# A fused attention, FFN and MoE kernel: four float64 weight chunks start their conversion on GpSimd, and the first block's order is rewritten

## The chip, the cores and the metric

The kernel runs on one core of one Trainium2 chip. The metric is the device time of one execution in microseconds (us), the median of three runs. The engines are TensorE (PE in the rows; PEld is its weight load), VectorE (DVE), ScalarE (ACT), GpSimd (POOL) and SyncE (SP), which here only starts transfers.

## The reference, cut to what matters

```python
scores = q @ k.T / sqrt(D); keep = is_global | is_local          # B=2, H=8, S=768, D=64
a = softmax(where(keep, scores - slope * dist, -1e9)); x = a @ v # -> x: 1536 x 512
h = x @ w_in                                                     # w_in: 512 x 2048
y = (h * tanh(softplus(h))) @ w_out                              # w_out: 2048 x 512
for e in range(4):                                               # four experts of width 1024
    out += p[:, e] * (relu(y @ w1[e]) @ w2[e])
```

All of it is to be float32, but `w_in` and `w_out` arrive as float64: the setup multiplies float32 random numbers by a float64 scalar. [...]

## The kernel before

The 1536 tokens are handled in three blocks of 512. A block goes through attention, the FFN (16 chunks of 128 hidden columns) and the experts. The later blocks overlap the attention of one block with the experts of another. The first block has nothing to overlap with, and this case is about it: `first_block` (line 788) issues its instructions in an order that is written out by hand, the string `PLAN` (line 42). Each letter is one step; the first occurrence of a letter is its step 0, the second its step 1, and so on, and the engines execute their own instructions in that order. I write a step as a letter and a number.

Attention of the first block has 16 pairs of heads. For pair k:

- S (TensorE): scores. X (VectorE, line 263): bias, and the row minimum, read from PSUM. E (ScalarE, line 274): exponentials. D (VectorE, lines 364 and 365): the inverse sums of two pairs.
- N (GpSimd) or V (VectorE), both line 370: the scaling of the probabilities, two instructions for a pair. T (TensorE): their transposes. C (ScalarE) or Z (VectorE), both line 380: the copy of the transposes out of PSUM. A (TensorE): probabilities times values.
- F (ScalarE) or G (VectorE), line 396: the copy of four pairs' results out of PSUM into `x0`, the input of the FFN.

Of the FFN of the first block, chunk c has the following steps.

- The raw chunk is 128 partitions x 1024 float64 (1 MB). It is fetched on SP's queue (line 563) into one of four buffers (`TURN`); two of them held queries and keys before. Chunk 0 is fetched at the very start, chunks 1 to 3 during attention, and chunk c+4 only when chunk c has been narrowed. The last two reuse buffers of chunks 12 and 13.
- a (ScalarE, line 584): reads every second 32-bit word, the upper half of each float64, scales it and writes float32. Three t steps (VectorE: line 587, then lines 589 and 591, which have two inputs from SBUF each) set the exponent and the mantissa. After the third t, SP writes the result to DRAM for the later blocks (line 593) and then starts the next fetch.
- H (TensorE, line 750): the hidden chunk. Then the activation `h * tanh(softplus(h))`: e (ScalarE exponential, line 643), c, n (VectorE), l (ScalarE logarithm and exponential, lines 662 and 663), u, m, v, g (VectorE, lines 667 to 682). P (TensorE, line 762): the product with `w_out`, accumulated over the 16 chunks.

At the end, w splits three expert chunks for the steps that follow, i and j and the digits begin block 1, and after P15 ScalarE and VectorE copy the result out (lines 743 and 744).

GpSimd has no instruction between 25.4 us and 152.6 us in the profile below. A step that waits holds up all that is behind it on its own engine: a waits for a fetch, and e and l stand behind it on ScalarE.

Of the kernel before, what the change touches and what calls it, by code (L numbers as in the profile page):

```python
# [12 lines left out]
AF = mybir.ActivationFunctionType  # L13
ALU = mybir.AluOpType

P = 128
# [8 lines left out]
NF1 = 16  # L25
# [6 lines left out]
TO_F32 = 2.0 ** -112  # L32
# [7 lines left out]


PLAN = (
    "SSYXXESYSEXSEDXNXESNTDCTXSENAZNEXATTSCZEDAXANSFSNEXTTDCNEZAXANTETSCZaADXNAtSFNTEXSCTXEAZSEDAVSVaXTTX"
    "CSEZAEADVVFTXTCEZAAaDVVTtTCaAZtAFtHtttteHcatntlHteaumcvnegacPtltumtHvngtlPteuamvcHgntltaPeucmtvgHntl"
    "tauPetmvgcPntltauHtmvgtePcnatltHutmteHvcagntltPeumavgHcntltuPetmcvnHgtlutPmevgcntlPumvgHtttePtcnlHau"
    "mtvtaHgetictnPetlcutHmwvgnwlPweuwcmvgHnwlwuwmPevcgnwlwPumvgj1P23456"
)

AFTER = {
# [473 lines left out]
class Body:  # L523
# [43 lines left out]
        self.w32[s] = self.wpool.tile([P, 1024], F32, tag="w", name=f"w{s}")  # L567
        self.nc.sync.dma_start(self.w32[s], (self.wts if kind == "moe" else self.wfirst if self.wide else self.wff)[n])

    def narrow(self, s):  # L570

        if s not in self.w64:
            return
        nc, raw = self.nc, self.w64.pop(s)
        word = raw.bitcast(I32).rearrange("p (n t) -> p n t", t=2)
        top = raw.bitcast(F32).rearrange("p (n t) -> p n t", t=2)[:, :, 1]
        if self.first:

            m = self.w32[s] = self.ring.tile([P, 1024], F32, tag="wl" if s % 2 else "wh", name=f"w{s}")
        else:
            m = self.w32[s] = self.wpool.tile([P, 1024], F32, tag="w", name=f"w{s}")
        nc.scalar.activation(m, top, AF.Abs, scale=TO_F32)
        yield
        mi = m.bitcast(I32)
        nc.vector.tensor_scalar(mi, mi, 0x0FFFFFFF, 3, ALU.bitwise_and, ALU.logical_shift_left)
        yield
        nc.vector.scalar_tensor_tensor(mi, word[:, :, 1], -0x40000000, mi, ALU.bitwise_and, ALU.bitwise_or)  # L589
        yield  # L590
        nc.vector.scalar_tensor_tensor(mi, word[:, :, 0], 29, mi, ALU.logical_shift_right, ALU.bitwise_or)
        if self.first:
            nc.sync.dma_start(self.wfirst[s], m)
# [194 lines left out]
    def first_block(self, ready, now):  # L788


        nc = self.nc
        pairs = [FirstPair(self, k) for k in range(TB // P * NP)]
        then = Attention(self, self.pair, 1)
        n = dict.fromkeys("SXEDNTCAFHecnlumvgPatw", 0)
        narrowing = [self.narrow(c) for c in range(NF1)]
        parts = [self.part(c) for c in range(NF1, NF1 + 3)]
        self.x0 = self.xy.tile([P, KC, TB], F32, tag="xyh", name="x0")

        for pair in pairs:
            pair.load()  # L800
            if pair.n == 9:
                now("fetch", 2)

        def ahead():
            while ready["fetch"] < NF1:
                c = ready["fetch"]
                before = [m for m in range(c) if TURN[m] == TURN[c]][-1:]
                if n["S"] < FREE.get(TURN[c], 0) or any(n["t"] < 3 * m + 3 for m in before):
                    break
                now("fetch", c + 1)  # L810

        def scores(k):
            pairs[k].scores()
            ahead()

        def warm(k):

            nc.tensor.matmul(self.bank(f"warm{k}", 0), self.ident, self.ident.unsqueeze(1).to_broadcast([P, 4, P]), start=True, stop=True)

        def inverse(k):  # L820
            assert n["E"] >= 2 * k + 2
            pairs[2 * k].inverse()

        def scale(engine):
            def run(k):
                assert n["D"] > k // 2
                pairs[k].scale(engine)
            return run

        def take(engine):  # L830
            def run(k):
                assert n["A"] >= 4 * k + 4
                pairs[4 * k].take(engine)
                ahead()
            return run

        def hidden(s):
            if s == 4:
                for c in range(NF1, NF1 + 3):
                    self.fetch(c)  # L840
            assert n["F"] == 4 and n["t"] >= 3 * s + 3
            self.accumulating = True
            self.hidden_first(s)
            ahead()

        def project(s):
            self.project_first(s)

        def begin(c):
            assert (c < 2 or n["A"] >= min(2 * c - 2, len(pairs))) and (c < 10 or n["P"] > c - 10)  # L850
            next(narrowing[c])

        def convert(k):
            c = k // 3
            assert n["a"] > c
            next(narrowing[c], None)
            ahead()

        def part(k):
            c, third = divmod(k, 3)  # L860
            assert ready["fetch"] >= NF1 and n["S"] == len(pairs) and n["P"] >= 8 + 2 * c
            if third == 0:
                ready["fetch"] = NF1 + 3
                next(parts[c])
            try:
                parts[c].send("vector" if third else None)
            except StopIteration:
                pass

        def begin_next(k):  # L870
            assert n["t"] >= 36
            then.load(4)

        pair = lambda stage, *args: lambda k: getattr(pairs[k], stage)(*args)
        ops = {
            "S": scores, "X": pair("biased"), "E": pair("exps"), "D": inverse, "N": scale(nc.gpsimd), "V": scale(nc.vector), "T": pair("trans"),
            "C": pair("copy", nc.scalar.copy), "Z": pair("copy", nc.vector.tensor_copy), "A": pair("av"),
            "F": take(nc.scalar.copy), "G": take(nc.vector.tensor_copy), "a": begin, "t": convert, "w": part,
            "Y": warm, "H": hidden, "e": self.mish_exp, "c": self.mish_cap, "n": self.mish_n, "l": self.mish_r,
            "u": self.mish_u, "m": self.mish_m, "v": self.mish_v, "g": self.gate_first, "P": project,  # L880
            "i": begin_next, "j": lambda k: then.split(k + 1),
            "1": lambda k: then.ahead(), "2": lambda k: then.scores(), "3": lambda k: then.softmax(),
            "4": lambda k: then.norm(), "5": lambda k: then.trans(), "6": lambda k: then.av(),
        }
        same = dict(Z="C", G="F", V="N")
        for token in PLAN:
            kind = same.get(token, token)
            for other in AFTER.get(kind, ()):
                assert n[other] > n[kind], (token, n[kind], other)
            ops[token](n.setdefault(kind, 0))  # L890
            n[kind] += 1
        ready["narrow"], ready["part"] = NF1, NF1 + n["w"] // 3
        return then, n["P"]
# [160 lines left out]
```

## Time and profile before

| | |
|---|---|
| median of 3 runs | 933.07 us (932.06 to 934.48) |
| the profiled execution: its own time | 934.25 us |
| the profiled execution: span in the profile | 932.4 us |
| busy over the span: TensorE, VectorE | 902.5 us, 532.8 us |
| busy over the span: ScalarE, GpSimd | 438.6 us, 370.3 us |
| mean granted TensorE clock | 0.993 |
| first block (to its last activation step) | 0 to 153.35 us |

The span runs from the first to the last instruction. Busy times are unions of an engine's instructions. Shares over the whole span mix two stages: from about 158 us on TensorE is busy almost without a gap, and before that it is not. The change lies in the first 153 us.

### The profile page before, as it was taken

Reading aid. Unit: us, or ns where it says so; the run is one execution under the profiler, and the core shown is the slowest. Engines: PE = TensorE matmul, PEld = TensorE weight load, DVE = VectorE, ACT = ScalarE, POOL = GpSimd, SP = SyncE. Lnnn points to the kernel's source line nnn. Section 1 sums busy time; section 2 is a strip of 40 time slices with the busy share of each in tenths; the row PEclk is TensorE's granted clock in tenths of the full one; section 3 lists DMA queues with packets and bytes.
Section 4 is the critical chain, followed back from the end, with each engine's and each line's share of the span. In section 5 each row is a group of like instructions: output and inputs, shape, how many; then the busy total and the mean of one; then the engine's idle time right before and its main releaser. Section 6 shows DMA issues by size and latency. Waiting matters only on the chain.

```text
span 932.4 us, 11519 instructions
## 1 busy us (share of the span) xinstructions
PE 902.5 (97%) x3962; PEld 689.6 (74%) x3962; DVE 532.8 (57%) x1057; ACT 438.6 (47%) x856; POOL 370.3 (40%) x379
## 2 busy tenths in 40 slices
PE   7889999999899999999999999999999999999997
PEld 4534444777688888877777888888888888888886
DVE  6989989776752188888777611248885121112122
ACT  6553436766553355666666643224445323423230
POOL 4000001775674445446766654400014444544440
PEclk9999999999899999999999999999999999999999
DMA  8477363534222578854444222055563243223201
GB/s 299 188 277 268 142 237 125 181 136 136 90 69 99 205 266 301 308 203 155 136 140 154 91 91 91 23 191 205 190 232 107 91 144 105 91 93 112 91 23 50
DMA packets 40373, 142.96 MB, mean 153 GB/s; under 512 B 4592, under 2 KB 7408, under 8 KB 38256
## 3 DMA queue, kind: packets, MB, share of 16 engines
q1 hardware_dynamic: 40160, 142.10, 43.2%
q8 instruction: 33, 0.54, 0.2%
q14 instruction: 36, 0.29, 0.1%
q10 hardware_dynamic: 144, 0.02, 0.0%
HBM read 113.80 MB, written 28.31 MB: 152 GB/s over the span
## 4 chain that ended last, share of the span: by engine, by line
PE 64%; DVE 19%; ACT 8%; DMA 4%; issue 3%; SPq 0%; POOL 0%; ACTq 0%; DVEq 0%; POOLq 0%
PE h L627 30%; PE acc L733 29%; DMA raw<-in_wff 2%; DVE kl L230 2%; DVE nr L672 2%; DVE e L667 2%; PE o L296 1%; DMA big<-in_wff 1%; ACT p L274 1%; PE pt L191 1%; DVE nr L678 1%; DVE w L589 1%; DVE n L655 1%; DVE e L682 1%; ACT wh L609 1%
## 5 line engine op out<-in xcount | busy, mean ns | idle before, releaser
L612 POOL TENSOR_TENSOR wl<-w,wh 128x512 fp32r<-128x512 f32 x218 | 289.7, 1350 | 324.5 <-ACT wh L609 312.1
L708 DVE SCALAR_TENSOR_TENSOR gl<-h,gh 128x512 fp32r<-128x512 f32 x96 | 66.2, 690 | 267.3 <-ACT gh L703 267.3
L609 ACT CAST wh<-w 128x1024 fp32r<-128x1024 f32 x112 | 117.6, 1050 | 113.6 <-PE acc L733 106.2
L733 PE MATMUL acc<-wh,gh 128*128 128x512 f32 (+1 forms) x384 | 151.3, 394 | 0.0
L733 PE MATMUL acc<-wh,gl 128*128 128x512 f32 (+1 forms) x384 | 148.9, 388 | 0.0
L733 PE MATMUL acc<-wl,gh 128*128 128x512 f32 (+1 forms) x384 | 148.8, 387 | 0.0
L703 ACT ACTIVATE gh<-h 128x512 fp32r<-128x512 f32 x96 | 57.3, 597 | 115.7 <-PE h L627 115.7
L733 PEld LDWEIGHTS acc<-wh,gl 128*128 128x128 f32 x384 | 72.1, 188 | 15.1
L733 PEld LDWEIGHTS acc<-wl,gh 128*128 128x128 f32 x384 | 72.2, 188 | 14.2
L733 PEld LDWEIGHTS acc<-wh,gh 128*128 128x128 f32 x384 | 72.2, 188 | 13.9
L239 POOL TENSOR_TENSOR v<-raw,v 128x256 fp32r<-128x256 f32 x32 | 27.4, 855 | 127.2 <-ACT v L238 127.2
L750 PE MATMUL h<-x,w 128*128 128x512 f32 x128 | 57.0, 593 | 0.7 <-ACT x L396 0.7
L186 POOL TENSOR_SCALAR p<-p,st 128x256 f32<-128x256 f32 (+1 forms) x64 | 30.0, 481 | 65.1 <-DVE st L184 63.8
L627 PE MATMUL h<-y0h,wh 128*128 128x512 f32 x128 | 52.8, 413 | 2.4 <-DVE st L263 1.5
L274 ACT ACTIVATE p<-t,st 128x256 f32<-128x256 f32 (+1 forms) x96 | 46.3, 484 | 13.7 <-DVE st L263 13.3
L627 PE MATMUL h<-y0l,wh 128*128 128x512 f32 x128 | 51.0, 399 | 0.0
L627 PE MATMUL h<-y0h,wl 128*128 128x512 f32 x128 | 51.0, 398 | 0.0
L627 PE MATMUL h<-y1h,wh 128*128 128x512 f32 x128 | 50.8, 397 | 0.1
L627 PE MATMUL h<-y1l,wh 128*128 128x512 f32 x128 | 49.9, 390 | 0.0
L733 PE MATMUL acc<-gh,wh 128*128 128x512 f32 x128 | 49.9, 390 | 0.0
L627 PE MATMUL h<-y1h,wl 128*128 128x512 f32 x128 | 49.9, 390 | 0.0
L627 PE MATMUL h<-y2h,wh 128*128 128x512 f32 x128 | 49.9, 390 | 0.0
(154 smaller groups left out, 1795.3 us busy)
## 6 DMA issues: line engine op xcount, KB each, us to landing
w<-in_wts SPq DMA_DIRECT2D x96, 512.0 KB, 3.5
raw<-in_qkv SPq DMA_DIRECT2D x32, 512.0 KB, 3.7
big<-in_wff SPq DMA_DIRECT2D x10, 1024.0 KB, 6.7
wfirst<-w SPq DMA_DIRECT2D x16, 512.0 KB, 3.0
w<-wfirst SPq DMA_DIRECT2D x16, 512.0 KB, 4.2
wkeep<-wh SPq DMA_DIRECT2D x16, 512.0 KB, 3.1
wkeep<-wl SPq DMA_DIRECT2D x16, 512.0 KB, 2.9
wh<-wkeep SPq DMA_DIRECT2D x16, 512.0 KB, 3.2
```

The costliest lines, as they stand in the source:

```text
L186: nc.gpsimd.tensor_scalar(self.p[:, j, 0:self.nk * P], self.p[:, j, 0:self.nk * P], st[:, 2 + j:3 + j], 0.0, ALU.mult, ALU.add)
L230: nc.vector.tensor_tensor(self.kl, self.k, self.kh.bitcast(F32), ALU.subtract)
L239: nc.gpsimd.tensor_tensor(vv[:, :, 1:3, :], v, vv.bitcast(F32)[:, :, 0:4:3, :], ALU.subtract)
L274: nc.scalar.activation(p[:, j, 0:n], t[:, j, 0:n], AF.Exp, bias=self.least[:, j:j + 1], scale=-1.0, accum_out=self.sum[:, j:j + 1])
L609: (nc.vector.tensor_copy if copy == "vector" else nc.scalar.copy)(hi, w)
L612: getattr(nc, engine or "gpsimd").tensor_tensor(lo[:, c], w[:, c], hi.bitcast(F32)[:, c], ALU.subtract)
L627: nc.tensor.matmul(ps, a[:, c], r[:, kc, :], start=m == 0, stop=m == 3 * KC - 1)
L667: nc.vector.scalar_tensor_tensor(e, n, 2.0, r, ALU.add, ALU.mult)
L703: self.nc.scalar.activation(gh, self.h[s], AF.Relu)
L708: nc.vector.scalar_tensor_tensor(gl, h, 0.0, gh.bitcast(F32), ALU.max, ALU.subtract)
L733: nc.tensor.matmul(acc[:, h], a, r, start=f == 0 and m == 0, stop=f == per - 1 and m == 2)
L750: self.nc.tensor.matmul(ps, self.w32[s][:, kc * P:(kc + 1) * P], self.x0[:, kc, :], start=kc == 0, stop=kc == KC - 1)
```

## The change

`narrow` gets an argument. If it is set, the first conversion instruction runs on GpSimd as a multiplication instead of on ScalarE. The sign bit, which the absolute value cleared, is cut off by the next step's mask anyway. A new letter q begins a chunk in that way; a still begins it on ScalarE. The new `PLAN` uses q for chunks 0 to 3, has 16 C and no Z, four G and no F, eight N and eight V (before: eight C, eight Z, four F, ten N, six V), and another order nearly throughout. The number of each other letter is the same.

```diff
 PLAN = (
-    "SSYXXESYSEXSEDXNXESNTDCTXSENAZNEXATTSCZEDAXANSFSNEXTTDCNEZAXANTETSCZaADXNAtSFNTEXSCTXEAZSEDAVSVaXTTX"
-    "CSEZAEADVVFTXTCEZAAaDVVTtTCaAZtAFtHtttteHcatntlHteaumcvnegacPtltumtHvngtlPteuamvcHgntltaPeucmtvgHntl"
-    "tauPetmvgcPntltauHtmvgtePcnatltHutmteHvcagntltPeumavgHcntltuPetmcvnHgtlutPmevgcntlPumvgHtttePtcnlHau"
-    "mtvtaHgetictnPetlcutHmwvgnwlPweuwcmvgHnwlwuwmPevcgnwlwPumvgj1P23456"
+    "SSYXXESYSEXSEDXNXESNTDCTXSENANTCXSCqEAATSDCEXNAGSENXTCTDXNACtESNAEXTqTCDSCVAVEXATGETSCDSCVVAXqAXETTt"
+    "CSCAXEqASGEDXVEVTTCDCVAVAtTTCtCAtAGtHttatHectntlHeuacmvangetPlctumvHgntltaPeucmvnHgltauPmetvcgHntlt"
+    "umPetavcgnPtltutaHmtvtgeHtcantlPteucmvaHngtltuPetmvcHgnatlttPeumvgcPtntltHumtvteHgctntlPeuacmvHgntlt"
+    "auPemvgcnPtiltutHmtvwgwePwcwnwlwHuwmwvwgeHcnluPemvcgnlPumvgj1P23456"
 )
...
-    def narrow(self, s):
+    def narrow(self, s, gpsimd=()):
...
-        nc.scalar.activation(m, top, AF.Abs, scale=TO_F32)
+        if gpsimd:
+
+            nc.gpsimd.tensor_scalar(m, top, TO_F32, 0.0, ALU.mult, ALU.add)
+        else:
+            nc.scalar.activation(m, top, AF.Abs, scale=TO_F32)
...
-        narrowing = [self.narrow(c) for c in range(NF1)]
+        on_gpsimd = []
+        narrowing = [self.narrow(c, on_gpsimd) for c in range(NF1)]
...
-        def begin(c):
-            assert (c < 2 or n["A"] >= min(2 * c - 2, len(pairs))) and (c < 10 or n["P"] > c - 10)
-            next(narrowing[c])
+        def begin(gpsimd):
+            def run(c):
+                assert (c < 2 or n["A"] >= min(2 * c - 2, len(pairs))) and (c < 10 or n["P"] > c - 10)
+                on_gpsimd[:] = [c] * gpsimd
+                next(narrowing[c])
+            return run
...
-            "F": take(nc.scalar.copy), "G": take(nc.vector.tensor_copy), "a": begin, "t": convert, "w": part,
+            "F": take(nc.scalar.copy), "G": take(nc.vector.tensor_copy), "a": begin(0), "q": begin(1), "t": convert, "w": part,
...
-        same = dict(Z="C", G="F", V="N")
+        same = dict(Z="C", G="F", V="N", q="a")
```

## Rows read from the trace of the kernel before

**Rows 1.** Busy time of each engine in stretches; PEclk is TensorE's granted clock.

```profile
23.17:39.05 15.88, 13.55 (x132) 8.97 (x128) 14.09 (x50) 12.93 (x35) 2.19 (x4) 1.00 0.32 131
39.05:56.92 17.87, 15.06 (x31) 6.55 (x32) 14.38 (x20) 7.53 (x11) 0.00 (x0) 0.90 0.80 299
56.92:153.35 96.43, 94.27 (x218) 40.78 (x216) 90.13 (x128) 39.51 (x58) 0.73 (x1) 1.00 0.55 201
```

**Rows 2.** VectorE's waits from 23.17 to 153.35 us: total, times, longest.

```profile
DVE e L667 <- ACT r L663: 6.4, 9, 2.2
DVE e L650 <- ACT e L643: 1.2, 2, 0.9
DVE t L263 <- PE s L353: 1.1, 3, 0.6
DVE w L587 <- ACT w L584: 0.8, 1, 0.8
DVE st L364 <- ACT p L274: 0.7, 2, 0.4
```

**Rows 3.** Groups of VectorE's instructions, 23.17 to 153.35 us: busy us, mean ns.

```profile
L591 DVE SCALAR_TENSOR_TENSOR w<-big,w 128x1024 int32<-128x1024 int32 x10 | 12.2, 1221 | 0.1
...
L587 DVE TENSOR_SCALAR w<-w 128x1024 int32<-128x1024 int32 x16 | 11.0, 688 | 0.8 <-ACT w L584 0.8
...
L370 DVE TENSOR_SCALAR p<-p,st 128x256 f32<-128x256 f32 x12 | 3.4, 350 | 0.2
L380 DVE COPY pt<-pt 128x512 f32<-128x512 f32 x4 | 2.8, 688 | 0.0
```

**Rows 4.** Timeline, 18 to 24 us: start, duration, [idle before, releaser].

```profile
18.04 0.42 DVE L263 CUSTOM_DVE_ANT_0 t<-s,bias 128x256 f32<-128x256 f32 x1 [2.12 <-PE s L353]
...
22.33 0.70 PE L353 MATMUL s<-qk 64*128 64x256 f32 x4 [0.54 <-DMA qk<-in_qk]
...
23.17 0.42 DVE L263 CUSTOM_DVE_ANT_0 t<-s,bias 128x256 f32<-128x256 f32 x1 [0.37 <-PE s L353]
```

**Rows 5.** Line 380 on ScalarE: ns least, median, most; first and last start.

```profile
L380 ACT COPY pt<-pt x8: 354/585/585, 12.4 to 36.4; 128x512 f32<-128x512 f32 x6, 128x256 f32<-128x256 f32 x2
```

**Rows 6.** GpSimd: four scalings in the timeline, and line 612 as Rows 5.

```profile
15.43 1.84 POOL L370 TENSOR_SCALAR p<-p,st 128x256 f32<-128x256 f32 x4 [1.45 <-DVE st L365]
...
L612 POOL TENSOR_TENSOR wl<-w,wh x218: 1265/1289/1749, 165.9 to 907.5; 128x512 fp32r<-128x512 f32 x109
```

**Rows 7.** Timeline: one VectorE line alone and beside GpSimd.

```profile
153.83 0.69 DVE L230 TENSOR_TENSOR kl<-raw,kh 128x512 fp32r<-128x512 f32 x1
...
250.44 1.67 DVE L230 TENSOR_TENSOR kl<-raw,kh 128x512 fp32r<-128x512 f32 x1
...
248.83 2.73 POOL L612 TENSOR_TENSOR wl<-w,wh 128x512 fp32r<-128x512 f32 x2 [0.27 <-ACT wh L609]
```

**Rows 8.** Timeline of fetches of chunks 4 and 6, their a steps, and line 563's landings.

```profile
39.51 0.38 SPq L563 DMA_DIRECT2D big<-in_wff  x1
...
46.46 1.18 ACT L584 ACTIVATE w<-big 128x1024 f32<-128x1024 f32 x1 [2.80 <-DMA big<-in_wff]
...
45.97 0.37 SPq L563 DMA_DIRECT2D raw<-in_wff  x1
...
54.59 1.13 ACT L584 ACTIVATE w<-raw 128x1024 f32<-128x1024 f32 x1 [2.09 <-DMA raw<-in_wff]
...
56.92 0.69 DVE L667 SCALAR_TENSOR_TENSOR e<-n,r 128x512 f32<-128x512 f32 x1 [2.23 <-ACT r L663]
...
DMA to landing us min/median/max: 5.2/6.5/11.0
```

**Rows 9.** Timeline of VectorE: two steps u, and the last g.

```profile
125.48 0.69 DVE L667 SCALAR_TENSOR_TENSOR e<-n,r 128x512 f32<-128x512 f32 x1 [1.35 <-ACT r L663]
...
140.65 0.69 DVE L667 SCALAR_TENSOR_TENSOR e<-n,r 128x512 f32<-128x512 f32 x1 [0.15 <-ACT r L663]
...
152.66 0.69 DVE L682 TENSOR_TENSOR gl<-r,h 128x512 f32<-128x512 f32 x1
```

More of the change, by code (lines that the diff above doesn't have):

```diff
@@ L42 @@
 PLAN = (
-    "SSYXXESYSEXSEDXNXESNTDCTXSENAZNEXATTSCZEDAXANSFSNEXTTDCNEZAXANTETSCZaADXNAtSFNTEXSCTXEAZSEDAVSVaXTTX"
-    "CSEZAEADVVFTXTCEZAAaDVVTtTCaAZtAFtHtttteHcatntlHteaumcvnegacPtltumtHvngtlPteuamvcHgntltaPeucmtvgHntl"
-    "tauPetmvgcPntltauHtmvgtePcnatltHutmteHvcagntltPeumavgHcntltuPetmcvnHgtlutPmevgcntlPumvgHtttePtcnlHau"
-    "mtvtaHgetictnPetlcutHmwvgnwlPweuwcmvgHnwlwuwmPevcgnwlwPumvgj1P23456"
+    "SSYXXESYSEXSEDXNXESNTDCTXSENANTCXSCqEAATSDCEXNAGSENXTCTDXNACtESNAEXTqTCDSCVAVEXATGETSCDSCVVAXqAXETTt"
+    "CSCAXEqASGEDXVEVTTCDCVAVAtTTCtCAtAGtHttatHectntlHeuacmvangetPlctumvHgntltaPeucmvnHgtltauPmetvcgHntlt"
+    "umPetavcgnPtltutaHmtvtgeHtcantlPteucmvaHngtltuPetmcvgHnatlttPeumvgcPtntltHumtvteHgctntlPeuacmvHgntlt"
+    "auPemvgcnPtiltutHmtvwgwePwcwnwlwHuwmwvwgeHcnluPemvcgnlPumvgj1P23456"
 )
```

## The prediction

> **What bounds the kernel now.** I read the busy time by stretches first. From 23.17 us to the end of the first block VectorE is busy for 14.09 + 14.38 + 90.13 = 118.6 of 130.2 us [rows 1]; ScalarE is busy for less than half of the time and GpSimd has nothing to do. TensorE shows as busy as VectorE, but its bars include waiting in a filled pipeline; what ends last is told by the waits. VectorE stands still for 11.6 us in all, of which the view of its waits names 10.2 us [rows 2], and 7.6 of these end with ScalarE: a step u that waits for l, or a step c that waits for e. So in this stage VectorE's own work sets the time, plus about 10 us in which ScalarE's answer comes too late. From about 158 us on the order of this change plays no part, so what the first block gains or loses I carry to the end one to one.
>
> The clock of this argument starts at X10. The scores of pair 10 waited for their queries and keys, which landed at 22.33, and VectorE's X10 follows at 23.17 [rows 4]. That transfer is queued by the loads ahead of the written order, so the change can't bring it forward. Ahead of it VectorE has slack (2.12 us before X8 alone [rows 4]).
>
> **The work on VectorE.** The new order has no Z (-8 copies), four G (+4 copies of 512 columns) and two more V. Over the whole block this is a saving, but only what lies behind X10 counts. Before, Z9, Z11, Z13, Z15, six V and t0 lie behind X10. After, G1, G2, G3, eight V and D4 do, and t0 has moved ahead of it. Terms:
>
> - four Z gone: 4 x 0.69 = -2.75 by line 380 [rows 3]
> - t0 gone ahead: -0.69 by line 587 [rows 3]
> - G1 to G3: the same read of 512 columns of PSUM, 3 x 0.69 = +2.06 [rows 3]
> - V8 and V9, which were N8 and N9 on GpSimd: 4 x 0.35 = +1.40 [rows 3]
> - D4: two instructions on four columns, put at +0.3, less than half of such a copy, because it has almost no columns.
>
> Sum +0.3 us. The four other Z, which looked like a gain, lay where VectorE waits for the queries and keys anyway. All other VectorE steps are the same in number.
>
> **What goes to ScalarE.** Eight more C at 0.585 each at most [rows 5] and four F and four a fewer (a takes 1.18 [rows 8]): it ends with less work than before. It was busy for 12.93 of the 15.88 us behind X10 [rows 1], and there it now has ten C where it had F1 to F3, a0 to a3 and four C; this covers the extra copies. Without that cover each C would hold up its A by 0.6 us.
>
> **q on GpSimd.** Nothing of before shows a 1024-column scaling there. Four 256-column ones take 1.84 us, and two two-input halves 2 x 1.29 = 2.58 [rows 6]. The nearer row is the first, the same operation with four starts instead of one; so I take 1.5 us, between 1.1 (if about half of each 0.46 us scaling is its start; an estimate from that row) and 2.6. q0 stands ahead of N4 on GpSimd's queue; N4 must wait for D2 in both versions, and T4 behind it waits for the late X8, which covers it. q1 to q3 have no N behind them. Their results are wanted by t3, t6 and t9, more than 10 us of VectorE work later. So their duration itself costs nothing.
>
> What they can cost is VectorE's time. Line 230 on VectorE takes 0.69 us alone and 1.67 us while GpSimd runs a pair of 1.3 us instructions: about 1 us lost to one instruction [rows 7]. X, G and the copies read PSUM; V and t read SBUF, and q2 and q3 (their chunks land in the middle of the attention part) meet V10, V11 and perhaps t1. Bounds: 0 if they meet none, 2 x 2.58 = 5.2 if both are lost in full to V or t. I take 0.6, since X12 and X13 stand in the same stretch.
>
> The Trainium skill, SBUF — State Buffer, section "Who interferes with whom", says that VectorE and GpSimd share a pair of SBUF ports which one instruction holds for its whole length, and that a VectorE instruction with two SBUF inputs or in a two-port mode stops for a GpSimd instruction that reads SBUF. It speaks against this change, and line 230 agrees with it. By it the upper bound would be the price whenever q starts first.
>
> **The waits.** Now what is late next. The end of t2 releases chunk 4's fetch. Before, it was issued at 39.51 and a4 began at 46.46, 6.95 us later [rows 8]. After, t3, t4, G3, t5, t6, t7, t8 follow t2 on VectorE: three of 0.69 and four of 1.22, 6.95 us [rows 3]. Then c0 needs e0; but e0 is now queued behind a4 on ScalarE (before, e0 came first). a4 ends at 0.4 (the write's issue) + 6.95 + 1.18 = 8.5, e0, a ScalarE pass over 512 columns as in [rows 5], at 9.1: c0 waits 2.2 us. Chunk 6's fetch took 54.59 - 45.97 = 8.6 us [rows 8]; with that, c2 (behind e2, behind a6) waits 0.4, u0 0.15, u1 0.3. In the attention part G1 and D5 wait 0.35 each, because T6 and T7 now stand behind S10 on TensorE. Up to u1 that is 3.8.
>
> Behind u1 the set of steps left is the same in both, only the order differs. A step u that directly follows its n waits 1.35 us for l, and one with 1.2 us of work in between 0.15 [rows 9]. Before, one of the first kind (u11) lies in this part; after, two do (u14 and u15, as the w steps have been used up earlier): 2.7, and two of the second kind 0.3. The a steps take 6.5 us from issue in the middle [rows 8]; by that, u6 (l6 is behind a11) waits 1.2, c3 0.3, u8 0.3, c12 (e12 behind a15) 0.6. Sum 5.4.
>
> In all 9.2 us of waits where 10.2 were: -1.0.
>
> **The sum.** +0.3 + 0.6 - 1.0 = -0.1 us. The profiled execution took 934.25 us (span 932.4 and 1.85 around it), so 934.15 for the like; the median of the runs shown is 933.07, 1.2 lower, and by it the forecast is 933.0 us. A difference under 0.3%, 2.8 us, can't be told from no change here.
>
> **The rivals.**
>
> - The transfers land early. The a steps wait on fetches, and the shortest landing of line 563 is 5.2 us [rows 8]. With it for all, c0 waits 0.45 instead of 2.2, the waits at c2, u1, u6, c3, u8 and c12 (3.1) are gone, and with q meeting nothing (-0.6): -5.4, 927.6 us. For it: chunk 4's and 5's fetches are released earlier, relative to H0, than before. Against it: in absolute time they are issued when they were, and that stretch has its transfer engines 80% busy [rows 1]. It counts as faster from half of this on.
> - The shared access of GpSimd and VectorE decides, slower. q2 and q3 last 2.6 us each and VectorE stands still for all of it: 5.2 instead of 0.6, 937.6 us. For it: line 230 [rows 7]. Against it: X12 and X13 read PSUM. It counts as slower once the loss is above 3.5 us.
> - The a steps hold up ScalarE longer. If chunk 4 takes chunk 6's 8.6 us and one of the later ones that instead of 6.5, c0 waits 1.65 more and u6 2.1 more: +3.75, 936.8 us. For it: 56.92, where u1 waited 2.23 us in just that way [rows 8]. Against it: fetches late in the block run alone.
> - The change does nothing for the time, because GpSimd and ScalarE were both off the path: this falls together with the forecast.
>
> **How the numbers follow.** Forecast, with the case of no effect: 0.57; its own range is 931 to 935.5: the waits at c0, u6 and c12 (4.0 together) may be half or one and a half of what I put them at. Early transfers 0.20, shared access 0.12, held-up ScalarE 0.11. That gives faster 0.20, within 0.3% 0.57, slower 0.23. The range for eight in ten leaves out the far ends of the first two rivals: 929.0 to 937.8 us.
>
> **What would show it.** Right: X10 on VectorE again at about 23.2; two more t steps done by the start of H0; c0 waiting some 2 us for e0 behind a4; u14 and u15 with 1.35 us each; V or t near q2 or q3 longer than before by some tenths. Wrong: X10 earlier than 22.5, VectorE's waits up to the last g under 6 or over 13 us, or a q above 2.6 us. The last g began at 152.66 [rows 9]; I expect it between 151 and 155. The prediction would also be wrong if TensorE's granted clock fell for longer than before (0.90 from 39.05 to 56.92 [rows 1]) inside the stage from 158 us on, where TensorE is the bound.

## The result, and the profile after

The changed kernel took 940.26 us (936.42 to 943.62, 11 runs) against 933.07 us (932.05 to 936.25, 11 runs): ratio 1.0062, 95% interval 1.0043 to 1.0082. By the ratio it is slower by 5.8 us (4.0 to 7.7), by the medians by 7.2; no measurable difference was forecast, and the median lies 2.5 us above the range. The 11 times of the changed kernel fall into five from 936.4 to 938.2 us and six from 940.3 to 943.6, and the median lies among the six, so the ratio is the better figure for the loss. From line 584 on, line numbers of the changed kernel are 4 higher than before: a is line 588 (q is 586), t 591, 593 and 595, the write 597, e 647, c 654, l 666 and 667, u 671, g 686, P 766.

The profiled execution took 940.26 us, with a span of 938.5. Busy time by stretches, from X10 to the end of the last g and from there to the end (columns: stretch, length, busy time of TensorE, its weight load, VectorE, ScalarE, GpSimd, granted clock, share of the DMA engines, GB/s):

```profile
22.98:159.83 136.85, 124.58 (x396) 57.58 (x394) 119.46 (x200) 57.82 (x102) 3.39 (x4) 0.99 0.54 197
159.83:938.50 778.67, 761.20 (x3472) 622.77 (x3472) 399.85 (x789) 363.56 (x704) 358.21 (x345) 0.99 0.40 140
```

The stretch behind the last g is 778.67 us long; before it was 932.4 - 153.35 = 779.05. So the whole loss arose in the first block and was carried on one to one. From X10 to the end of the last g VectorE is busy for 119.46 us, where 118.6 were [rows 1]; the stretch has grown from 130.18 to 136.85 us. So VectorE's work grew by 0.9 us and its standing still from 11.6 to 17.4 us. The view of VectorE's waits in this stretch (total, times, longest) says for whom:

```profile
DVE e L654 <- ACT e L647: 9.3, 4, 5.1
DVE e L671 <- ACT r L667: 5.7, 8, 1.4
DVE t L263 <- PE s L353: 2.0, 1, 2.0
DVE st L364 <- ACT p L274: 0.3, 1, 0.3
DVE x L396 <- PE o L391: 0.2, 1, 0.2
```

Against [rows 2], u waits no longer than before (5.7 for 6.4). It is c, waiting for e, that went from 1.2 to 9.3 us, and one wait is 5.1 us of it. (The 2.0 at line 263 is X10's own wait; it ends at 22.98, so it is no part of the 17.4 us.) VectorE's timeline places them (start, duration, then idle time before and what ended it):

```profile
22.98 0.42 DVE L263 CUSTOM_DVE_ANT_0 t<-s,bias 128x256 f32<-128x256 f32 x1 [2.04 <-PE s L353]
...
46.31 0.43 DVE L654 TENSOR_SCALAR e<-e 128x512 f32<-128x512 f32 x1 [0.87 <-ACT e L647]
...
56.80 0.43 DVE L654 TENSOR_SCALAR e<-e 128x512 f32<-128x512 f32 x1 [2.81 <-ACT e L647]
...
77.07 0.43 DVE L654 TENSOR_SCALAR e<-e 128x512 f32<-128x512 f32 x1 [5.09 <-ACT e L647]
...
103.79 0.69 DVE L671 SCALAR_TENSOR_TENSOR e<-n,r 128x512 f32<-128x512 f32 x1 [1.39 <-ACT r L667]
...
152.17 0.69 DVE L671 SCALAR_TENSOR_TENSOR e<-n,r 128x512 f32<-128x512 f32 x1 [1.36 <-ACT r L667]
...
157.09 0.69 DVE L671 SCALAR_TENSOR_TENSOR e<-n,r 128x512 f32<-128x512 f32 x1 [1.36 <-ACT r L667]
...
159.14 0.69 DVE L686 TENSOR_TENSOR gl<-r,h 128x512 f32<-128x512 f32 x1
```

The first three waits of line 654 are c0, c2 and c4. The last g begins at 159.14, where it began at 152.66 [rows 9]: 6.5 us later. c2 waits for e2 and c4 for e4, and ScalarE's timeline shows what these stand behind: a6 (ahead of e2) and a8 (ahead of e4) wait for fetches.

```profile
55.14 1.14 ACT L588 ACTIVATE w<-raw 128x1024 f32<-128x1024 f32 x1 [2.62 <-DMA raw<-in_wff]
...
75.43 1.12 ACT L588 ACTIVATE w<-big 128x1024 f32<-128x1024 f32 x1 [6.92 <-DMA big<-in_wff]
76.44 0.60 ACT L647 ACTIVATE e<-h 128x512 f32<-128x512 f32 x1
```

ScalarE stands still for 6.92 us until chunk 8 has landed. In the kernel before the same a8 began at 68.60, 0.91 us after the work ahead of it, and c4 (line 650 there) waited for 0.91 us:

```profile
68.60 1.15 ACT L584 ACTIVATE w<-big 128x1024 f32<-128x1024 f32 x1 [0.91 <-DMA big<-in_wff]
...
70.27 0.43 DVE L650 TENSOR_SCALAR e<-e 128x512 f32<-128x512 f32 x1 [0.91 <-ACT e L643]
```

SP's queue of the changed kernel says when that fetch went out (the write of chunk 4's result, three expert chunks, chunk 8's fetch):

```profile
63.74 0.33 SPq L597 DMA_DIRECT2D wfirst<-w  x1
64.16 1.73 SPq L568 DMA_DIRECT2D w<-in_wts  x3
65.98 0.38 SPq L563 DMA_DIRECT2D big<-in_wff  x1
```

And SP's queue of the kernel before, at the same step:

```profile
62.32 0.33 SPq L593 DMA_DIRECT2D wfirst<-w  x1
62.74 0.38 SPq L563 DMA_DIRECT2D big<-in_wff  x1
63.21 1.86 SPq L568 DMA_DIRECT2D w<-in_wts  x3
```

The two have changed places. t14 frees chunk 4's buffer, but the next fetch is not issued by t14: it goes out at the next step that looks ahead (`ahead()`, called by t, S, F, G and H). Before, this was t15. In the new order H4 stands between t14 and t15. (In the diff ahead of the prediction the new `PLAN` is misprinted in two places. This t15 is missing there: the kernel has `PeucmvnHgtlta` for `PeucmvnHglta`. Further on it has `PetmcvgHna` for `PetmvcHgna`.) H4 does this (cut; the comments are mine):

```python
def hidden(s):
    if s == 4:
        for c in range(NF1, NF1 + 3):
            self.fetch(c)          # three expert chunks, 0.5 MB each
    ...
    ahead()                        # only here: chunk 8's fetch
```

So chunk 8 goes out 1.8 us later, behind 1.5 MB that nobody needs before w, and lands 75.43 - 65.98 = 9.45 us after its issue; before it took 68.60 - 62.74 = 5.86. Of the chain of waits between 60 and 80 us, followed back from its end, nearly half is this one transfer (shares by line, as the view prints them):

```profile
by line: DMA big<-in_wff 46.8%; PE acc L766 18.6%; SPq L568 6.2%; DVE w L593 6.1%; ACT w L588 5.6%; issue 4.2%; DVE gl L686 3.8%; DVE r L682 3.5%; DVE n L661 3.4%; DVE w L591 3.1%; ACT e L647 2.5%; DVE e L654 2.1%; SPq L563 0.1%; ACTq L588 
...
```

### The profile page after: what moved, and what is told of

It reads as the page before. It is cut to its first block, busy times and chain, and to the rows that moved or that the text cites. A ratio compares the mean times of both kernels' runs of the same rounds, so it can differ in the third digit from the quotient of the medians.

```text
span 938.5 us, 11522 instructions
## 1 busy us (share of the span) xinstructions
PE 904.2 (96%) x3962; PEld 689.5 (73%) x3962; DVE 532.4 (57%) x1057; ACT 435.7 (46%) x856; POOL 373.4 (40%) x379
## 4 chain that ended last, share of the span: by engine, by line
PE 68%; DVE 17%; ACT 7%; DMA 4%; issue 2%; SPq 0%; ACTq 0%; DVEq 0%
PE h L631 30%; PE acc L737 29%; PE acc L766 3%; PE h L754 2%; DMA big<-in_wff 2%; DVE kl L230 2%; DVE nr L676 2%; DVE e L671 1%; PE o L296 1%; ACT p L274 1%; DVE nr L682 1%; PE pt L191 1%; DVE n L659 1%; DVE e L686 1%; DVE n L652 1%
```

## The experiments

The theory after this reading: the place of H4 in front of t15, and with it SP's order, costs nearly all of the loss; q on GpSimd costs next to nothing. The rivals: q's shared access to SBUF, or the new order as a whole (waits of l and e behind a). Each result below stands beside the kernel before on the same chip: 932.98 us (24 runs) for e1 to e4, 932.6 (35) for e5 to e8, 932.48 (23) for e9 to e12. Waits and landings come from one profiled execution of each kernel, times from all runs.

### One part at a time

**e1_fetch8_first.** The changed kernel, with SP's order restored inside H4.

```diff
             if s == 4:
+                ahead()
                 for c in range(NF1, NF1 + 3):
```

> The new kernel with one edit: in the step H4 the fetch of chunk 8 is issued before the three expert chunks instead of after them. Theory A (SP's queue): the changed order put H4 in front of t15, so the three expert chunks (1.5 MB) went out at 64.16 us ahead of chunk 8's fetch at 65.98; a8 stood until 75.43 and c4 waited 5.1 us. Then chunk 8 lands some 3 to 4 us sooner, c4 waits under 1.5 us, and the time falls by 3 to 4.5 us, to about 936. Theory B (chunk 8 is late anyway, because its release by t14 is late): the wait moves to another step and the time falls by less than 1 us.

933.28 us (12 runs), ratio 1.0011 (0.9999 to 1.0023). One line gives back 7.0 us by the medians (4.8 by the ratios), more than the 3 to 4.5 expected. SP's queue and ScalarE's a8 in this kernel:

```profile
60.90 0.38 SPq L563 DMA_DIRECT2D big<-in_wff  x1
61.37 1.85 SPq L568 DMA_DIRECT2D w<-in_wts  x3
...
66.74 1.18 ACT L588 ACTIVATE w<-big 128x1024 f32<-128x1024 f32 x1 [1.49 <-DMA big<-in_wff]
```

Chunk 8 lands within 5.84 us, c4 waits for nothing, and the last g begins at 152.61.

**e2_experts_first.** The opposite: the kernel before, with the expert fetches moved ahead of chunk 8's.

```diff
-            if s == 4:
-                for c in range(NF1, NF1 + 3):
-                    self.fetch(c)
...
+            if k == 15:                      # in the t step, ahead of its ahead()
+                for m in range(NF1, NF1 + 3):
+                    self.fetch(m)
```

> The kernel before with one edit: the three expert chunks are issued ahead of chunk 8's fetch, as the new order has it. Theory A: c3, which stands behind e3 and a8, waits 3 to 5 us more than its 0.91, and the time rises by 3 to 4.5 us, to 936 to 937.5. Theory B: within 1 us of before.

938.16 us (6 runs), ratio 1.0052 (1.0036 to 1.0068). The old order, with a on ScalarE throughout, loses 5.2 us by this swap alone (4.9 by the ratio). Chunk 8 took 8.83 us from issue to a8. VectorE's waits name line 650, and its timeline has one long wait of that line, at c4 (the expectation calls it c3):

```profile
DVE e L650 <- ACT e L643: 5.7, 1, 5.7
```

**e3_q_in_old_order.** The changed code with the old PLAN, in which only the first four a are q.

> The kernel before with one edit: the first four chunks begin on GpSimd, in the old order, with q where a stood. It tells the price of GpSimd's part alone. Theory C (the shared access of VectorE and GpSimd costs): V or t near q lengthens by 0.5 to 1.3 us in sum, and the time rises by 0.5 to 1.5 us. Rival (ScalarE's relief decides in the attention part): the E and C steps come earlier by up to 1.2 us each and the time falls by 1 to 2 us.

933.64 us (11 runs), ratio 1.0004 (0.9996 to 1.0013): GpSimd's part by itself changes nothing that can be measured, though a V pair beside q lasted 2.02 us instead of 1.14.

**e4_a_in_new_order.** The new PLAN with a for every q.

> The new kernel with one edit: a in place of each q, so that all chunks begin on ScalarE, in the new order. Theory C: V10 and V11 take 1.14 instead of 2.03 us and t1 1.22 instead of 1.68, 1.35 us saved, of which ScalarE's four more instructions take back up to 1: the time is 0 to 1.5 us lower. Rival (GpSimd's part is what made the new kernel slower): the time falls by 4 us or more.

936.46 us (7 runs), ratio 1.0048 (1.0030 to 1.0065). It is lower than the changed kernel by 3.8 us by the medians and by 1.3 by the ratios, between the two forecasts, and its interval overlaps that of the changed kernel (1.0043 to 1.0082): by itself this doesn't tell whether q costs something there. Chunk 8 still goes out behind the experts, takes 7.88 us, and c4 waits 3.54 us. e9 asks the question again in an order without that fault.

### The queue's order, and how much of it

**e8_t15_before_H4.** The changed kernel with one letter of PLAN moved.

```diff
-...vangetPlctumvHgntltaPeucmvnHgtltauPmetvcgHntlt"
+...vangetPlctumvHgntltaPeucmvngtHltauPmetvcgHntlt"
```

> The new kernel with one letter of the order moved: H4 goes from in front of t15 to behind it, no other edit. t15's release puts chunk 8's fetch ahead of the three expert chunks on SP's queue. If SP's queue is the cause (theory A), this gives what the edit in the step H4 gave, 933 to 934.5 us. If it was the edit itself that helped in some other way (the rival), the time stays at 937 or more.

932.57 us (12 runs), ratio 1.0001 (0.9990 to 1.0011), a little under what was expected: the rival is out. The fetch stands ahead of the experts again and c4 doesn't wait. The profiled execution is the slowest of the twelve (936.9 us); other waits are long in it, which "What stays open" uses.

**e11_one_expert_first.** The changed kernel with one expert chunk ahead of chunk 8's fetch and two behind it.

> The new kernel with one edit: of the three expert chunks only one (0.5 MB) is issued ahead of chunk 8's fetch, the two others behind it. A dose of theory A: three ahead cost 5 to 7 us, none ahead 0. If the price goes with the bytes that are ahead, one costs 1 to 2.5 us over the run with chunk 8 first (933.3): 934 to 935.5, and c4 waits 1 to 2 us. If it is a matter of order alone (the rival: whatever is second loses the whole time), it is 938 or more.

934.6 us (12 runs), ratio 1.0018 (1.0002 to 1.0034), as expected. ScalarE's a8 and VectorE's c4:

```profile
69.95 1.14 ACT L588 ACTIVATE w<-big 128x1024 f32<-128x1024 f32 x1 [3.08 <-DMA big<-in_wff]
...
71.61 0.43 DVE L654 TENSOR_SCALAR e<-e 128x512 f32<-128x512 f32 x1 [1.26 <-ACT e L647]
```

With no, one and three expert chunks ahead of chunk 8's fetch (e1, e11, the changed kernel), chunk 8 takes 5.84, 6.95 and 9.45 us from issue to a8, ScalarE waits ahead of a8 for 1.49, 3.08 and 6.92, c4 waits 0, 1.26 and 5.09, and the ratio is 1.0011, 1.0018 and 1.0062. The intervals of the first two overlap: the step from none to one shows in the waits, not in the times.

**e7_experts_late_old_order.** The kernel before, with the expert fetches at H10 instead of H4.

```diff
-            if s == 4:
+            if s == 10:
```

> The kernel before with one edit: the three expert chunks are fetched at H10 instead of H4. Theory A: chunk 8's and 9's fetches no longer share the transfer engines with them; c3's wait of 0.91 us goes and the time falls by 0.5 to 1.5 us. Rival: chunk 8 leads the queue already, nothing waits on chunk 9, and the time stays within 0.5 us.

933.15 us (12 runs), ratio 1.0001 (0.9990 to 1.0011). c4's wait fell from 0.91 to 0.55 us, but the time didn't: in the old order, once chunk 8 goes first, no difference can be measured by where the experts' 1.5 MB lie.

### What a better order is worth

**e5_a_behind_l.** e1, and nine a steps moved behind the e or l steps that had to wait behind them on ScalarE: a4 behind l0, a6 behind l1, a7 behind e3, a8 behind e4, a10 behind e6, a11 behind l6, a12 behind l7, a13 behind l8, a15 behind e12. The lines with the moves of a4 and a10 (a6 leaves its place in the first):

```diff
-...tAGtHttatHectntlHeuacmvange...
+...tAGtHtttHectntlaHeuacmvnge...
-...nPtltutaHmtvtgeHt...
+...nPtltutHmtvtgeaHt...
```

> The new kernel with chunk 8's fetch first, and nine of the twelve a steps from chunk 4 on put behind the l or e step that they stood ahead of, so that ScalarE doesn't stand at a fetch while VectorE waits for l or e. Theory D (what is left of VectorE's waits comes from a ahead of e and l): the waits for c0, c2, u6 and u7 (0.17, 0.90, 0.96 and 1.59 us in the run with the fetch first) go, and the time falls by 2 to 3.5 us, to 930 to 931.5. Rival (the fetches are late as such, so the first t of the chunk waits instead): within 1 us of 933.3.

930.11 us (12 runs), ratio 0.9977 (0.9967 to 0.9987). VectorE's waits, u and c:

```profile
DVE e L671 <- ACT r L667: 3.3, 5, 1.4
DVE e L654 <- ACT e L647: 2.0, 4, 0.8
```

Both kinds together are 5.3 us, where the changed kernel had 15.0 and e1 9.0.

**e9_a_for_q_best_order.** e5 with a for every q.

> The run with the a steps behind l (930.1) with a in place of each q: ScalarE begins all chunks. What GpSimd's part is worth in an order that has no other fault. Theory C (what VectorE loses at the shared access, 0.9 us in one V and 0.5 in one t, is as much as ScalarE's relief gives): within 1.5 us of 930.1. Rival (ScalarE has no room in the attention part): 932 or more.

930.53 us (11 runs), ratio 0.9977 (0.9968 to 0.9986), the same ratio as e5. Together with e3: in the old order and in this one, who begins the first four chunks is worth nothing that can be measured.

**e6_all_three.** e5, the experts at H10, and the last two w steps moved between l14 and u14 and between l15 and u15.

> As the run with the a steps behind l, and besides the three expert chunks are fetched at H10 instead of H4, when the transfer engines are idle, and w7 and w8 stand between l14 and u14 and between l15 and u15. Theory: the two waits of 1.36 us at the end shrink to 0.75 each (-1.2 us), chunk 9's fetch lands sooner (-0.5): 1 to 2 us below the run without these. Rival: the transfers that move to H10 collide with chunks 14 and 15, and the gain is gone.

930.77 us (12 runs), ratio 0.9978 (0.9967 to 0.9988): nothing beyond e5. The waits at u14 and u15 did fall from 1.36 to 0.76 us each, but c14's rose from 0.61 to 1.57: with VectorE earlier, e14 waits for H14 on TensorE. The gain moved one step on.

**e12_best.** e1 and e5's moves but with a4 behind e1, w as in e6, and H14 and H15 moved forward.

> The run with the a steps behind l, with a4 behind e1, w7 and w8 between l and u of chunks 14 and 15, and H14 and H15 ahead of P12 and behind P12, because c14 waited 1.57 us for e14, which waited for H14 on TensorE. Theory: c1's 0.83 goes, the waits of u14 and u15 shrink by 0.6 each and c14's goes: 1.5 to 3 us below 930.1. Rival: H14 ahead delays P12 and with it the accumulation, and the last g comes no earlier.

929.4 us (5 runs), ratio 0.9962 (0.9949 to 0.9975). It is 0.7 below e5, less than the 1.5 to 3 expected; the intervals of the two overlap.

**e10_a_behind_l_old_order.** The kernel before, without q, with eight a steps moved in the same way (a4 behind l0, a6 behind l1, a8 behind e4, a9 behind e5, a10 behind e6, a11 behind l6, a12 behind l7, a13 behind l8).

> The kernel before with eight a steps put behind the l or e step that they stood ahead of. Theory D: the waits of u1 (2.23 us), c3 (0.91) and u6 (1.00) shrink to a few tenths each and the time falls by 2 to 3.5 us against before. Rival (the gain belongs to the new order): within 1 us of before.

928.72 us (5 runs), ratio 0.9953 (0.9940 to 0.9966), a little better than expected, and the lowest median of all kernels here (its interval overlaps e12's). VectorE's waits, which answer to [rows 2] line by line:

```profile
DVE e L667 <- ACT r L663: 2.3, 6, 1.4
...
DVE w L587 <- ACT w L584: 0.8, 1, 0.8
DVE st L364 <- ACT p L274: 0.7, 2, 0.4
DVE e L650 <- ACT e L643: 0.3, 1, 0.3
```

u waits 2.3 instead of 6.4 us and c 0.3 instead of 1.2: 5.0 us less, and the kernel is 3.8 us faster. (The 0.3 is c4's, which the expectation calls c3.)

## Why the prediction was wrong

**The step that failed** is in "The waits": "Behind u1 the set of steps left is the same in both, only the order differs", and the price of every a behind it, "6.5 us from issue in the middle". By that no wait at c4 was in the sum. The set of steps is the same, but not the order in which their transfers enter SP's queue: H4 issues three fetches, and moving t15 behind H4 put chunk 8's fetch behind them. It went out 1.8 us later, behind the experts, and took 9.45 us, 3.6 more than in e1: 5.4 us late in all. By as much ScalarE's wait ahead of a8 grows, from 1.49 us in e1 to 6.92, and c4, which doesn't wait in e1, waits 5.09. e1 undoes nothing but this and e8 undoes it by moving H4, and both remove the loss; e2 makes the old kernel slow with nothing but this; e11's waits lie between. That is the cause, shown from both sides. The size is less fixed: behind the same three loads chunk 8 took 7.88 us (e4), 8.83 (e2) and 9.45.

The Trainium skill, DMA: Bandwidth & Descriptors, section "Queues, rings and completion order", says that each DMA engine takes descriptors up in the order of the ring. The runs agree: with no, one and three transfers just ahead of it on SP's queue chunk 8 took 5.84, 6.95 and 9.45 us.

**The other terms, one by one:**

- *What bounds the kernel now*: VectorE and its waits for ScalarE, as read. Of the 10.2 us that [rows 2] names, 9.1 end with ScalarE, not 7.6: the lines of 587 and 364 name it too.
- *What goes to ScalarE*: less work, as said: it is busy for 57.82 us of the stretch where it was for 59.97. (a0 began at 22.24 before, just ahead of X10 and not behind it.)
- *X10 again at 23.2*: right, 22.98. It is no fixed time, though: in the profiles of the kernels with the new order it lies between 21.8 (e9) and 23.7 (e8).
- *VectorE's work, +0.3 and +0.6 of shared access*: the sum was right, +0.86 measured for +0.9, but by luck. The parts were not: shared access is 1.35 (V10 and V11 0.89, t1 0.46) and the rest -0.5 for +0.3.
- *Waits, 9.2*: 15.5 by the sum of the single waits. Right or nearly: the attention part 0.53 for 0.7, u0 and u1 0.37 for 0.45, u6 0.85 for 1.2, u10 and u13 0.37 for 0.3, u14 and u15 2.72 for 2.7. Mis-sized: c0 0.87 for 2.2 (chunk 4 landed within 5.6 us), c2 2.81 for 0.4 (chunk 6 took 9.24 us, not 8.6, and c2 came earlier), c3, u8 and c12 nothing for 1.2, u7 1.39 for nothing (l7 stands behind a12, which waited for its fetch), c14 0.54 for nothing. Missing: c4's 5.09.
- *One to one behind the last g*: right, 778.67 for 779.05 us, with TensorE's granted clock at 0.99.
- *q 1.5 us, between 1.1 and 2.6*: 1.12 to 1.22 us, near the lower bound. An estimate from it and [rows 6]: 0.46 us for 256 columns and about 1.15 for 1024 in one instruction give a start of 0.23, half of the 0.46, as the lower bound had it.

**The rivals.** "The a steps hold up ScalarE longer" was right in kind and in sign, but named c0 and u6 (3.75 us, 936.8 us). Those two waited 1.7 us together, where by it they wait 7.2; the loss came at c4, by a mechanism it hadn't named. What stood against it, "fetches late in the block run alone", did not hold for chunk 8's fetch. "The transfers land early" came true for some (chunks 4, 10, 11 and 13 took 5.4 to 5.6 us) and not for chunks 5, 6 and 8 (8.6, 9.24 and 9.45). Shared access did not decide: 1.35 us in the profile, nothing that can be measured in the timed kernels (e3, e9). "Nothing for the time" fell with the forecast. The prediction's own sign of being wrong, waits over 13 us, was met, and the last g at 159.14 lies outside its 151 to 155.

**What stays open.** By the ratios the swap costs 4.9 us in the old order (e2) and 4.8 to 5.7 in the new one (1.0062 against 1.0011 and 1.0001), which agrees with c4's waits of 5.7 and 5.1. By the medians it is 5.2 and 7.0 to 7.7; by those the new order would lose some two microseconds more, and by the ratios nothing that can be told from noise. In single profiles c2's wait differs too, and the swap isn't the cause, since c2 lies ahead of it in time and e8, without the swap, has the long wait as well. The changed kernel's 2.81 us stands above; e8 and then e1:

```profile
58.91 0.43 DVE L654 TENSOR_SCALAR e<-e 128x512 f32<-128x512 f32 x1 [2.42 <-ACT e L647]
53.54 0.43 DVE L654 TENSOR_SCALAR e<-e 128x512 f32<-128x512 f32 x1 [0.90 <-ACT e L647]
```

e4 and e11, with expert chunks ahead of chunk 8, have 0.87 and 0.78. Where c2 waited long, chunk 5 took 8.6 us from issue to its a step; in the three others at most 7.2. Why it lands late in some executions no experiment tested. Whether q costs something in the changed order itself (e4) stays open as well.

## What to carry to other kernels

When a step moves in a written order, list every queue that it passes: a transfer is issued where the program next looks ahead, not where its buffer becomes free, and a bulk load that nobody needs soon must not stand in front of one that somebody waits for. A step that may wait for a transfer goes behind the short steps that others wait for on the same engine: eight such moves gained 0.47% in the old kernel. Here, moving work off an engine that wasn't the bound gained nothing that could be measured, and the reordering that came with it lost 0.6%.

## What the runs showed of the hardware

Two VectorE steps met q and lasted longer. GpSimd's timeline shows the four q (line 586), with q2 and q3 last:

```profile
14.16 1.19 POOL L586 TENSOR_SCALAR w<-big 128x1024 f32<-128x1024 f32 x1
...
22.17 1.12 POOL L586 TENSOR_SCALAR w<-big 128x1024 f32<-128x1024 f32 x1
28.10 1.22 POOL L586 TENSOR_SCALAR w<-raw 128x1024 f32<-128x1024 f32 x1 [4.81 <-DMA raw<-in_wff]
30.49 1.13 POOL L586 TENSOR_SCALAR w<-raw 128x1024 f32<-128x1024 f32 x1 [1.18 <-PE pt L191]
```

Beside them, VectorE's V10 and V11 (four instructions), t1, and another four V later, undisturbed:

```profile
27.69 2.03 DVE L370 TENSOR_SCALAR p<-p,st 128x256 f32<-128x256 f32 x4
...
31.02 1.68 DVE L593 SCALAR_TENSOR_TENSOR w<-big,w 128x1024 int32<-128x1024 int32 x1
...
34.86 1.14 DVE L370 TENSOR_SCALAR p<-p,st 128x256 f32<-128x256 f32 x4
```

By line, with ns least, median, most:

```profile
L370 DVE TENSOR_SCALAR p<-p,st x16: 342/347/1237, 24.2 to 37.1; 128x256 f32<-128x256 f32 x16
```

Of the four V at 27.69, one took 1.237 us where the median is 0.347: it lost 0.89 us beside a q of 1.22 us that lay wholly within the four. t1 took 1.68 us instead of 1.22. V has only one tensor as input. The Trainium skill, SBUF — State Buffer, section "Who interferes with whom", says that such a scaling can run in a two-port mode, and that of it and a GpSimd instruction the one that comes second then waits; these rows agree. In e1, with the same four q, V10, V11 and t1 lost nothing, and q3, which met a t1 already running, lasted 1.33 us:

```profile
26.85 1.14 DVE L370 TENSOR_SCALAR p<-p,st 128x256 f32<-128x256 f32 x4
29.28 1.22 DVE L593 SCALAR_TENSOR_TENSOR w<-big,w 128x1024 int32<-128x1024 int32 x1
30.20 1.33 POOL L586 TENSOR_SCALAR w<-raw 128x1024 f32<-128x1024 f32 x1 [1.18 <-DMA raw<-in_wff]
```

So the 1.35 us is what one execution happened to lose; in e1's it is 0.

TensorE's clock fell after the stall of 5 us. Three stretches of the changed kernel (columns as above):

```profile
70.00:75.00 5.00, 4.90 (x12) 1.71 (x10) 1.99 (x3) 0.00 (x0) 0.00 (x0) 1.00 1.00 406
75.00:80.00 5.00, 1.99 (x4) 0.96 (x4) 2.89 (x5) 2.85 (x5) 0.00 (x0) 0.86 0.45 176
80.00:85.00 5.00, 4.06 (x7) 1.34 (x6) 5.00 (x9) 1.54 (x3) 0.00 (x0) 0.80 0.27 99
```

The granted clock is 1.00 (2.4 GHz) up to 75 us. TensorE is then busy for only 1.99 of 5 us, and the mean falls to 0.86 and 0.80, so part of this time was granted 1.2 GHz. From 80 to 85 us it cost nothing visible: VectorE is busy for all of it and is the bound there. The first row also shows the transfer engines full (share 1.00, 406 GB/s) while chunk 8 is on its way.
